# A Conformer block on one core: the first two query groups attend in two key halves, the front is ordered by its first chunk, two VectorE exponentials are in flight, and dummy matmuls stand in TensorE's waits

## The chip, the cores and the metric

The kernel runs on one core of a Trainium2 chip. The metric is the device time of one execution in microseconds (us). Before the change it was 1018.75, 1017.7 and 1015.3 us in three runs, a median of 1017.7 us. The profile is one further execution.

The core has five engines, each with its own in-order stream of instructions: TensorE (PE: matmuls into the accumulators in PSUM, with its weight loads shown apart as PEld), VectorE (DVE), ScalarE (ACT), GpSimd (POOL) and SyncE (SP, which only issues DMAs here). They wait for each other with semaphores.

## The reference, cut to what matters

B = 2 sequences of T = 4000 tokens with D = 144 features, H = 4 heads of 36, FF = 576, a depthwise convolution over 5 tokens; all in bfloat16.

```
h = layernorm(x);  x = x + 0.5 * (silu(h @ w_ff1a) @ w_ff1b)
h = layernorm(x);  q, k, v = heads(h @ w_qkv)
p = softmax(q @ k^T / 6);  x = x + (p @ v) @ w_o
h = layernorm(x) @ w_pw1;  h = h[:, :D] * sigmoid(h[:, D:])
c = depthwise_conv5(h);    x = x + silu(c) @ w_pw2
h = layernorm(x);  x = x + 0.5 * (silu(h @ w_ff2a) @ w_ff2b)
return layernorm(x)
```

Attention is the bulk: 2 x 4 x 4000 x 4000 scores, each of which needs an exponential.

## The kernel before

**Tiling.** The 8000 tokens are 16 chunks `c` of 500 (8 per sequence; CPB = 8), each chunk 4 blocks of 125 tokens. A chunk is also a query group. Keys come in 63 tiles of 64 (NT = 63), so attention is 16 x 63 = 1008 tiles, in the order of the list `its` (chunk, then key tile). One tile holds all four heads, in 128 partitions by 1000 columns:

- four score matmuls (`PS<-QT,KT`) fill two PSUM banks out of six (0 to 5) that all work shares;
- the exponential goes to one of the slots of the ring `PT` (NPT = 7). It is made by ScalarE in one instruction (`ACTIVATE PT<-PS 128x1000`), or by VectorE in eight (`dve_tile`, line 981, over the buffers `ZB` and `MB`): two that turn scores into a scaled integer (`ZB<-PS`), five that split it into exponent and mantissa and work out a polynomial, and a product that writes `PT`. At most one such VectorE tile is under way;
- four matmuls (`PS<-PT,VA`) add the tile's share of p @ v, with a column of ones that gives the softmax sum, into banks 6 and 7 (BX = 6), which no other work may use before the end.

After a chunk's last tile `epilogue` (line 927) copies banks 6 and 7 to `OTF` in one VectorE instruction, transposes it on TensorE (`PS<-IDF,OTF`), and normalises it to `AN`. Then `post1` does w_o, a layernorm and the gated product, and `post2` the convolution, w_pw2, the second feed-forward, the last layernorm and the store. A chunk's `pre` (line 755) is the first feed-forward (`ff1`: layernorm to `XN`, transposes by `IDENT` to `XT`, matmuls `PS<-XT,WA` and `PS<-XT,WE`, the silu to `HT`, matmuls `PS<-WB,HT`) and then `pre2` (line 730: layernorm, transposes to `XTQ`, projections to `KT`, `VA`, `QT`).

**Who sets the order.** The Python code does not write engine streams directly. Each piece of work is a generator (a thread) that asks for an engine, a bank or a slot (`need`), and `Rec.op` (line 67) records an instruction and estimates its end from a table of costs. `pick` (line 1071) chooses what is recorded next: scores "S", a ScalarE exponential "E", a p @ v "O", or a thread "T"; score matmuls are put off until `act_end() - 0.48`, the time at which ScalarE would run dry. `due` (line 1144) starts a VectorE tile. `replay` then writes the per-engine streams with semaphores, so that nearly all instructions of the profile carry one helper's line, L158; tiles are told apart by their names.

**Front and tail.** Until keys and values of all 8 chunks of the first sequence are made (`kv_done`), the mode is "front": a query group may only use the key tiles that are there, and no VectorE tile may start. The first group, chunk 0, needs all 63 key tiles, and with them the keys of chunks 1 to 7, before chunk 1 can begin (its sums would need banks 6 and 7). Chunks 0 and 1 use the silu of ScalarE's table (NSILU = 2), the later ones tanh, which shares a table with the exponential; changing tables is an `ACT_TABLE_LOAD`. In layernorms VectorE makes mean and variance (`ST`, `MV`), GpSimd adds epsilon and takes the power -0.5 (`RS`); `XN` is written by VectorE in front and tail, by GpSimd between. After the last exponential the mode is "tail": what is left is chunk 15's epilogue, `post1` and `post2`, beside the end of chunk 14's.

**Start.** The inputs' DMAs go out on SP (`X` of chunks 0 to 7, then other weights) and on ScalarE's queue (group w0: `WA`, `WE`, `WB`; group w1: `WQKV`). VectorE sets buffers to zero, then `setup_qk` (line 476) copies `WQKV` to the padded `WQ` and `WK`, and then the layernorm statistics begin. TensorE begins with 36 matmuls (NWARM) of a zeroed `PT` slot, whose results nobody uses.

Of the kernel before, what the change touches and what calls it, by code (L numbers as in the profile page):

```python
# [6 lines left out]
ALU = mybir.AluOpType  # L7
# [7 lines left out]
DH = 36  # L15
# [33 lines left out]
class Rec:  # L49
# [8 lines left out]
    def __init__(self, nc):  # L58
        self.nc = nc
        self.ops = []  # L60
        self.n = {}
        self.hist = {}
        self.free = {e: 1.0 for e in self.ENGS}
        self.kind = None
        self.last = 0.0

    def op(self, eng, name, *a, r=(), w=(), q=None, cost=0.1, kind=None, lat=None, **k):
# [4 lines left out]
        o.idx = self.n.get(lane, 0)  # L72
        self.n[lane] = o.idx + 1
# [11 lines left out]
        start = self.free[eng]  # L85
        for d, raw in o.deps:
            if d.eng != eng or d.q is not None or (raw and eng != "pe"):
                start = max(start, d.done + self.SEM[eng])
# [6 lines left out]
        o.done = start + cost + ((self.LAT[eng] if lat is None else lat) if q is None else 2.0)  # L95
# [213 lines left out]
def bass_standalone__conformer_family_zipformer__speech_kernel(  # L309
# [30 lines left out]
    NPT = 7  # L340
    NU = 5
    NAN = 5
    ND = 1
    NWARM = 36
    NSILU = 2
# [3 lines left out]
    ALONE = 2  # L349
    OFREE = 3  # L350
# [3 lines left out]
    LATE = 0.3  # L354
    DGAP = 4.0
# [8 lines left out]
    NHALF = sb("NHALF", [NB], F32)  # L364
    XT = sb("XT", [NXT, 2, CH])
# [8 lines left out]
    ZB = sb("ZB", [ND, 2, CH], U16)  # L374
    MB = sb("MB", [ND, 2, CH], U16)
# [32 lines left out]
    ZBF = ZB[:, :, :, :].rearrange("p a b n -> p (a b n)").bitcast(BF16).rearrange("p (a n) -> p a n", a=ND)  # L408
    MBH = MB[:, :, :, :].rearrange("p a b n -> p (a b n)").bitcast(F16).rearrange("p (a n) -> p a n", a=ND)

# [3 lines left out]
    def load(eng, q, dst, src, w):  # L414
        op(eng, "dma_start", dst, src, q=q, w=w, cost=0.7)
# [4 lines left out]
    def load_x(eng, c):  # L420
        load(eng, f"x{c}", X[0:TB, c * NB:(c + 1) * NB, :], x_tok[c], [("X", c, i) for i in range(NB)])

    def load_ff(eng, q, WA, WE, WB, wa, wb, nm):
        load(eng, q, WA[0:HD, :, :], kh(wa)[:, :, 0:512], [(nm, "a", 0)])
        load(eng, q, WE[0:HD, :, 64:128], kh(wa)[:, :, 512:FF], [(nm, "a", 1)])
        load(eng, q, WB[:, 0:4, :], wb[0:512, :].rearrange("(t p) d -> p t d", p=128), [(nm, "b", 0)])
        load(eng, q, WB[0:64, 4, :], wb[512:FF, :], [(nm, "b", 1)])
        load(eng, q, WB[64:128, 5, :], wb[512:FF, :], [(nm, "b", 2)])

    op("dve", "memset", WP2Z[:, :, :], 0.0, w=[("WP2Z", i) for i in range(NB)])  # L430
    load_x("sp", 0)
    load_ff("act", "w0", WA1, WE1, WB1, w_ff1a, w_ff1b, "W1")
    load("act", "w1", WQKV[0:HD, :, :], kh(w_qkv), ["WQKV"])
    for c in range(1, CPB):
        load_x("sp", c)
# [6 lines left out]
    load_ff("sp", "w2", WA2, WE2, WB2, w_ff2a, w_ff2b, "W2")  # L442
# [3 lines left out]
    op("dve", "memset", PT[:, 0, :, :], 0.0, w=[("PT", 0)])  # L446
# [3 lines left out]
    op("pool", "memset", NHALF[:, :], -0.5, w=["NHALF"])  # L450
    for WE, WB, nm in ((WE1, WB1, "W1"), (WE2, WB2, "W2")):
# [19 lines left out]

    for i in range(NWARM):
        op("pe", "matmul", PSV[:, i % 8, 0:CH], lhsT=PT[:, 0, 0, 0:128], rhs=PT[:, 0, 0, 0:CH], start=True, stop=True,
           r=[("PT", 0)], w=[("ps", i % 8)], cost=0.3)

    def setup_qk():
        for Wt, nm, o0 in ((WQ, "WQ", 0), (WK, "WK", D)):
            for k in range(2):
                op("dve", "tensor_copy", Wt[0:HD, k, :, 0:DH],
                   WQKV[0:HD, k, o0:o0 + D].rearrange("p (h d) -> p h d", h=H), r=["WQKV", nm + "0"], w=[nm],  # L480
                   cost=0.15)
# [4 lines left out]
    xnp, xtp, thp, htp, swp, anp, ptp, dzp = (  # L486
        Slots(R, range(n)) for n in (NXN, NXT, NTH, NHT, NSW, NAN, NPT, ND))
# [65 lines left out]
    def ln(c, bs):  # L553
# [8 lines left out]
        yield need("pool")  # L562
        op("pool", "tensor_scalar", RS[0:TB, u, 1, 0:n], MV[0:TB, u, 0:n, 1], LN_EPS, None, op0=ALU.add,
# [663 lines left out]
```

## Time and profile before

| what | value |
|---|---|
| median of three runs | 1017.7 us (1015.3 to 1018.75) |
| the profiled execution, its own time | 1012.16 us |
| its span in the trace | 1010.4 us (1.76 us lie around it) |
| mean granted TensorE clock | 0.976 |
| exponential tiles on ScalarE / VectorE | 906 / 102 |
| first exponential begins / last one ends | 39.32 / 964.65 us |

The page of the profile gives busy times by engine, the span in 40 slices, the chain of work that ended last, and the costliest groups of instructions. A group row reads: line, engine, operation, output tile<-input tiles, shapes, count | busy us, mean ns of one | idle time of the engine before them and what ended it. Since ScalarE's instructions overlap at their ends, the mean of one can be above busy time divided by count. A timeline row reads: start, duration, engine, line, operation, shapes, count, and in brackets the idle time before it with what ended it. A row of windows reads: the stretch, its length, busy time of PE, PEld, DVE, ACT and POOL with the number of instructions, the granted clock of TensorE, the DMA share and GB/s; where only PE was asked for, only its busy time stands there. The page's row PEclk is that clock in tenths for each slice, 9 being 90% or more.

### The profile page before, as it was taken

What the parts mean: (1) busy time and instruction counts of PE and PEld (TensorE: products, weight loads), DVE (VectorE), ACT (ScalarE), POOL (GpSimd) and SP (SyncE); (2) the same over time, 40 slices, a digit from 0 to 9 for tenths busy, and PEclk for the clock granted to TensorE, in tenths of its full rate; (3) what the DMA queues carried; (4) which work ended last, traced back from release to release, by engine and by line L of the source; (5) the groups of instructions that cost most, each with busy time, mean ns of one, the idle gap of its engine ahead of it and who ended that gap; (6) DMA issues with size and microseconds to landing.
All of it is one profiled execution on the core that took longest, in us unless ns stands there. A gap on an engine that the chain in (4) does not pass through costs nothing.

```text
span 1010.4 us, 26729 instructions
## 1 busy us (share of the span) xinstructions
PE 920.5 (91%) x11294; PEld 400.8 (40%) x11294; DVE 824.1 (82%) x2160; ACT 932.0 (92%) x1163; POOL 288.8 (29%) x563
## 2 busy tenths in 40 slices
PE   8999899999999999999999998799898998989865
PEld 4544244433444444434434343233333333334343
DVE  5976878997988888988879878888878887878745
ACT  3898889999999999999999999999999999999933
POOL 3321314324324325133523321111222231313213
PEclk8999989999999999999999999999999999999967
DMA  4000000000000000000000000000000000000000
GB/s 129 5 2 2 2 2 2 2 2 2 2 2 3 7 8 7 1 2 8 8 2 2 8 7 7 2 2 7 1 3 6 2 7 1 8 2 7 1 7 12
DMA packets 7290, 7.32 MB, mean 7 GB/s; under 512 B 2344, under 2 KB 7170, under 8 KB 7170
## 3 DMA queue, kind: packets, MB, share of 16 engines
q1 hardware_dynamic: 6014, 5.14, 1.7%
q8 instruction: 88, 1.44, 0.6%
q10 hardware_dynamic: 1156, 0.47, 0.2%
q14 instruction: 32, 0.26, 0.1%
HBM read 3.31 MB, written 2.30 MB: 6 GB/s over the span
## 4 chain that ended last, share of the span: by engine, by line
ACT 47%; PE 33%; DVE 12%; POOL 6%; issue 1%; DMA 1%; ACTq 0%; POOLq 0%; DVEq 0%
ACT PT L158 41%; PE PS L158 33%; ACT TH L158 6%; POOL XN L158 3%; POOL RS L158 3%; DVE MB L158 2%; DVE ZB L158 2%; DVE ST L158 2%; DVE X L158 1%; DVE HT L158 1%; DVE XT L158 1%; DMA WQKV<-in_w_qkv_dram 1%; DVE MV L158 1%; DVE PT L158 0%; DVE OTF L158 0%
## 5 line engine op out<-in xcount | busy, mean ns | idle before, releaser
L158 ACT ACTIVATE PT<-PS 128x1000 bf16<-128x1000 f32 x906 | 841.0, 1054 | 13.4 <-PE PS L158 12.0
L158 PE MATMUL PS<-QT,KT 64*64 64x500 bf16 x4032 | 419.9, 387 | 28.2 <-ACT PT L158 22.2
L158 PE MATMUL PS<-PT,VA 64*37 64x500 bf16 x4032 | 355.5, 376 | 16.5 <-ACT PT L158 13.3
L158 POOL TENSOR_SCALAR RS<-MV 125x4 f32<-125x4 f32 (+1 forms) x159 | 50.1, 315 | 643.1 <-DVE MV L158 637.8
L158 PEld LDWEIGHTS PS<-QT,KT 64*64 64x64 bf16 x4032 | 125.5, 104 | 225.8 <-ACT PT L158 146.6
L158 DVE TENSOR_SCALAR ZB<-PS 128x500 uint16<-128x500 f32 x204 | 137.7, 675 | 54.0 <-PE PS L158 50.1
L158 PEld LDWEIGHTS PS<-PT,VA 64*37 64x37 bf16 x4032 | 114.9, 95 | 132.1 <-ACT PT L158 49.1
L158 POOL TENSOR_SCALAR XN<-X,RS 125x144 bf16<-125x144 bf16 x232 | 124.6, 549 | 6.1
L158 ACT ACTIVATE TH<-PS 128x500 bf16<-128x500 f32 (+2 forms) x200 | 104.4, 549 | 10.0 <-PE PS L158 9.3
L158 POOL TENSOR_TENSOR RS<-RS,NHALF 125x4 f32<-125x4 f32 (+1 forms) x101 | 100.6, 996 | 8.4
L158 DVE SCALAR_TENSOR_TENSOR HT<-TH,PS 128x500 bf16<-128x500 bf16 (+1 forms) x140 | 83.4, 616 | 17.1 <-ACT TH L158 15.9
L158 DVE TENSOR_SCALAR MB<-MB 128x1000 f16<-128x1000 f16 x204 | 84.7, 415 | 1.7
L158 DVE SCALAR_TENSOR_TENSOR X<-PS,X 125x288 bf16<-125x288 f32 x128 | 57.2, 453 | 35.3 <-PE PS L158 34.3
L158 PE MATMUL PS<-XT,WA 72*128 72x500 bf16 x256 | 76.9, 396 | 4.7 <-DVE HT L158 3.1
L158 DVE BATCH_NORM_STATS2 ST<-X 125x6 f32<-125x144 bf16 x320 | 75.2, 293 | 0.2
L158 DVE TENSOR_TENSOR PT<-ZB,MB 128x1000 bf16<-128x1000 bf16 x102 | 70.6, 692 | 2.4
L158 DVE TENSOR_TENSOR MB<-MB 128x1000 f16<-128x1000 f16 x102 | 69.0, 676 | 2.1
L158 PE MATMUL PS<-WB,HT 128*125 128x144 bf16 x640 | 63.4, 239 | 1.1 <-ACT HT L158 0.7
L158 PEld LDWEIGHTS PS<-WB,HT 128*125 128x125 bf16 x640 | 49.3, 142 | 28.6 <-issue 18.6
L158 PE MATMUL PS<-IDENT,XN 125*72 125x125 bf16 x512 | 44.1, 227 | 17.8 <-DVE XN L158 9.0
L158 DVE COPY XT<-PS 72x1000 bf16<-72x1000 bf16 (+1 forms) x67 | 41.2, 616 | 17.7 <-PE PS L158 16.8
L158 PEld LDWEIGHTS PS<-IDENT,XN 125*72 125x72 bf16 x512 | 32.9, 116 | 39.8 <-POOL XN L158 14.4
(78 smaller groups left out, 687.0 us busy)
## 6 DMA issues: line engine op xcount, KB each, us to landing
X<-in_x_dram SPq DMA_DIRECT2D x16, 140.6 KB
out_dram<-XN SPq DMA_DIRECT2D x14, 140.6 KB
out_dram<-XN SPq DMA_DIRECT2D x4, 70.3 KB
WA<-in_w_ff1a_dram ACTq DMA_DIRECT2D x1, 144.0 KB
WB<-in_w_ff1b_dram ACTq DMA_DIRECT2D x1, 144.0 KB
WA<-in_w_ff2a_dram SPq DMA_DIRECT2D x1, 144.0 KB
WB<-in_w_ff2b_dram SPq DMA_DIRECT2D x1, 144.0 KB
WQKV<-in_w_qkv_dram ACTq DMA_DIRECT2D x1, 121.5 KB
```

The lines of the kernel that those rows point to most:

```text
L158: ins = getattr(eng, o.name)(*o.a, **o.k)
```

## The change

**Two key halves.** The list of tiles is built from `phases`: (chunk 0, key tiles 0 to 38), (chunk 1, 0 to 38), (chunk 0, 39 to 62), (chunk 1, 39 to 62), then chunks 2 to 15 whole (`NQ` = 2, `HALF` = 5 chunks of keys, 39 tiles). After a first half, `epilogue` copies banks 6 and 7 to `SAVE` (fp32, in space of `QT` that belongs to the second sequence) and ends; after the second half `OTF` is the sum of the banks and `SAVE`. Query projections that would overwrite `SAVE` wait until it has been read. Two chunks' queries, not one, are projected early.

**VectorE tiles.** `ZB` and `MB` go; a VectorE tile works in place in two slots of `PT`, of which there are now 9. Two tiles may be under way (`LIVE` = 2), the second from when the first has taken its scores (`early`); a tile near the end of its phase goes ahead of other threads (rank -1). They may begin in the front once 4 chunks of keys are made (`FDVE`). There are 899 exponentials on ScalarE and 109 on VectorE.

**Front.** Chunk 0's threads have rank -1 and go ahead of others that could begin up to `FIRST` = 0.3 earlier, until the first exponential. Only chunk 0 uses the silu table (`NSILU` = 1); tiny activations of `DUM` bring the silu table in at the start and the exponential's table after chunk 0's first feed-forward. `setup_qk` moves from VectorE to GpSimd and into `pre2` of chunk 0. The DMA of `X` for chunk 1, and with it all behind it on SP, waits for `WA` and `WE`; `WB` gets a queue of its own (w3). In front and tail, epsilon is added by VectorE, not GpSimd. On ScalarE, 146 `TH` (tanh) instructions of 500 columns stand where there were 142, 12 `HT` (silu) where there were 16; between the first and the last exponential it has 8 more `TH` of 500 columns, one more of 250, and on balance three more copies from PSUM.

**Dummy matmuls.** The 36 start matmuls become 50 of `IDENT` by `IDENT`, 128 columns. In `Rec.op`, `filler` puts more of them wherever TensorE is expected to wait over 0.12 us, until the first exponential (169 of them in all by then) and again in the tail (245). They write bank 7.

**Numbers of the planner.** The costs of DMAs, scores, p @ v, `XN_COST` and the power change, and scores are put off until `act_end() - AHEAD` with 0.64 in the place of 0.48.

The core of the diff:

```diff
@@ Rec.op
-        start = self.free[eng]
+        start = ready = self.free[eng]
...
+        if eng == "pe" and self.filler is not None and not self.filling:
+            self.filling = True
+            for _ in range(int((ready - start - 0.12) / 0.056)):
+                self.filler()
...
-    NPT = 7
+    NPT = 9
-    NWARM = 36
-    NSILU = 2
+    LIVE = 2
+    NWARM = 50
+    NSILU = 1
+    NQ = 2
+    FDVE = 4
+    SOON = 3
+    AHEAD = 0.64
+    HALF = 5
+    FIRST = 0.3
...
+    load_x("sp", 0)
+    load_ff("act", "w0", "w3", WA1, WE1, WB1, w_ff1a, w_ff1b, "W1", 3.5, 4.5)
+    load("act", "w1", WQKV[0:HD, :, :], kh(w_qkv), ["WQKV"], lat=5.0)
+    for c in range(1, CPB):
+        load_x("sp", c, [("W1", "a", 0), ("W1", "a", 1)] if c == 1 else ())
...
+    def warm(cost=0.056, bk=BX + 1, n0=0):
+        op("pe", "matmul", PSV[:, bk, n0:n0 + 128], lhsT=IDENT[:, :], rhs=IDENT[:, :], start=True, stop=True, r=["ID"],
+           w=[("ps", bk)], cost=cost, kind="f")
+
     for i in range(NWARM):
-        op("pe", "matmul", PSV[:, i % 8, 0:CH], lhsT=PT[:, 0, 0, 0:128], rhs=PT[:, 0, 0, 0:CH], start=True, stop=True,
+        warm(0.1, BX + i % 2, i // 2 % 4 * 128)
+    R.filler = warm
...
-                op("dve", "tensor_copy", Wt[0:HD, k, :, 0:DH],
+                op("pool", "tensor_copy", Wt[0:HD, k, :, 0:DH],
...
+        if silu and mode["front"] and c == NSILU - 1:
+            op("act", "activation", DUM[:, :], NHALF[:, 0:1], ACT.Exp, bias=0.0, scale=1.0, r=["NHALF"], w=["DUM"],
...
+    def epilogue(c, part):
+        if part:
+            op("dve", "tensor_copy", SAVE[:, c, :, :], ps, r=rk, w=[("SAVE", c), "OREL"], cost=c_dve(2 * CH))
...
+        if c < NQ:
+            op("dve", "tensor_tensor", OTF[:, :, :], ps, SAVE[:, c, :, :], op=ALU.add, r=rk + [("SAVE", c)],
...
+    phases = [(c, t0, t1) for t0, t1 in ((0, tiles_by(HALF - 1)), (tiles_by(HALF - 1), NT)) for c in range(NQ)]
+    phases += [(c, 0, NT) for c in range(NQ, NCH)]
...
-        deadline = act_end() - 0.48
+        deadline = act_end() - AHEAD
...
-        if n >= NIT or not DVE_EXP or len(kv_done) < CPB or live_dve[0] >= 1 or lag():
+        if n >= NIT or not DVE_EXP or live_dve[0] >= LIVE or early[0] or lag():
...
     mode["tail"] = True
-    for i in (BX, BX + 1):
-        banks.free[i] = R.last
+    banks.free[BX] = R.last
+    R.filler = warm
```

What this does to three places of the engine streams follows. A row is an instruction, or several alike in succession; "waits" names the semaphore that the first of them waits for.

**TensorE at the start.** Before, the start matmuls are followed by chunk 0's and chunk 1's transposes (`IDENT,XN`) and feed-forward:

```order
L158 MATMUL PS<-PT 128x500 x36
L158 MATMUL PS<-IDENT,XN 72x125 x12
L158 MATMUL PS<-XT,WA 128x500 x8
L158 MATMUL PS<-XT,WE 128x250 x4
L158 MATMUL PS<-IDENT,XN 72x125 x8
L158 MATMUL PS<-WB,HT 125x144 x20
```

Now:

```order
L167 MATMUL PS<-IDENT 128x128 x106
L167 MATMUL PS<-IDENT,XN 72x125 x4
L167 MATMUL PS<-IDENT 128x128 x2
L167 MATMUL PS<-IDENT,XN 72x125 x4
L167 MATMUL PS<-IDENT 128x128 x9
L167 MATMUL PS<-XT,WA 128x500 x8
L167 MATMUL PS<-XT,WE 128x250 x4
L167 MATMUL PS<-IDENT,XN 72x125 x4
L167 MATMUL PS<-IDENT 128x128 x8
L167 MATMUL PS<-WB,HT 125x144 x20
```

Chunk 1's transposes no longer stand ahead of chunk 0's first feed-forward matmul, and dummies fill the places between.

**VectorE at the start**, behind its memsets. Before, with s_q_w1, s_q_x0 to s_q_x2 the arrivals of `WQKV` and of `X` of chunks 0 to 2:

```order
L158 COPY WQ<-WQKV 72x4x36 [waits s_q_w1]
L158 COPY WQ<-WQKV 72x4x36
L158 COPY WK<-WQKV 72x4x36 x2
L158 BN_STATS ST<-X 125x6 [waits s_q_x0]
L158 BN_STATS ST<-X 125x6 x3
L158 BN_AGGR MV<-ST 125x2 [waits s_dve] x4
L158 BN_STATS ST<-X 125x6 [waits s_q_x1]
L158 BN_STATS ST<-X 125x6 x3
L158 BN_AGGR MV<-ST 125x2 [waits s_dve] x4
L158 BN_STATS ST<-X 125x6 [waits s_q_x2]
L158 BN_STATS ST<-X 125x6
L158 TENSOR_SCALAR XN<-X,MV,RS 125x144 [waits s_pool]
```

Now:

```order
L167 BN_STATS ST<-X 125x6 [waits s_q_x0]
L167 BN_STATS ST<-X 125x6 x3
L167 BN_AGGR MV<-ST 125x2 [waits s_dve] x2
L167 TENSOR_SCALAR RS<-MV 125x2 [waits s_dve]
L167 BN_AGGR MV<-ST 125x2 x2
L167 TENSOR_SCALAR RS<-MV 125x2 [waits s_dve]
L167 BN_STATS ST<-X 125x6 [waits s_q_x1]
L167 BN_STATS ST<-X 125x6
L167 TENSOR_SCALAR XN<-X,MV,RS 125x144 [waits s_pool]
```

The weight copies are gone from VectorE, so its first wait is for `X` of chunk 0; the first `XN` now stands behind the arrival of chunk 1's `X`, whose DMA on SP waits for `WA` and `WE`.

**TensorE at the last tiles.** Before, the last p @ v matmuls are followed by the epilogue's transposes:

```order
L158 MATMUL PS<-WB,HT 125x144 x5
L158 MATMUL PS<-PT,VA 37x500 x8
L158 MATMUL PS<-IDF,OTF 125x128 x8
L158 MATMUL PS<-IDENT,AN 72x125 x8
L158 MATMUL PS<-WO,XT 125x144 x8
L158 MATMUL PS<-IDENT,XN 72x125 x8
```

Now (`WB,HT` here is the end of chunk 14's second feed-forward):

```order
L167 MATMUL PS<-PT,VA 37x500 x8
L167 MATMUL PS<-IDENT 128x128 x26
L167 MATMUL PS<-IDF,OTF 125x128 x4
L167 MATMUL PS<-WB,HT 125x144 x15
L167 MATMUL PS<-IDF,OTF 125x128 x4
L167 MATMUL PS<-WB,HT 125x144 x5
L167 MATMUL PS<-IDENT 128x128 x9
L167 MATMUL PS<-IDENT,AN 72x125 x8
```

26 dummies now stand between the last p @ v and the transposes, and since they write bank 7, the first of them waits, like the transposes, for the VectorE copy to `OTF` that reads that bank. Chunk 14's matmuls stand between the two groups of transposes.

More of the change, by code (lines that the diff above doesn't have):

```diff
@@ L683, in proj @@
         cc = c % CPB
[L684 removed]
+        over = nm == "WQ" and p == 1 and c >= CPB
+        bk = yield need("pe", banks, dur=0.42, cond=(lambda: not saved) if over else None)
         for k in range(2):
@@ L689, in proj @@
         yield need("dve", hold=True)
-        copy(dst, PSV[:, bk, 0:CH], [("ps", bk)], [(nm + "T", c)], CH)
+        copy(dst, PSV[:, bk, 0:CH], [("ps", bk)], [(nm + "T", c)] + [("SAVE", i) for i in range(NQ) if over], CH)
         banks.give(bk)
@@ L1167, in bass_standalone__conformer_family_zipformer__speech_kernel @@
             live_dve[0] += 1
+            early[0] += 1
+            owed[0] += 2
             last_dve[0] = R.free["pe"]
-            S.add(dve_tile(n), R.free["pe"] - 0.3, first=True, rank=3)
+            th = S.add(dve_tile(n), R.free["pe"] - 0.3, first=True, rank=3)
+            tiles.append((th, n - its[n][2] + phases[its[n][0]][2]))
+        for th, end in tiles:
+            if n_s[0] >= end - SOON:
+                th.rank = -1
         banks.keep = KEEP
```

213 lines of the change are left out of this document (123 added, 90 removed).

## The prediction

> **What bounds the kernel now.** I read the page first, then windows by stage, then the groups, then the timeline of the first 40 us and of the end. From the page:
>
> ```profile
> span 1010.4 us, 26729 instructions
> PE 920.5 (91%) x11294; PEld 400.8 (40%) x11294; DVE 824.1 (82%) x2160; ACT 932.0 (92%) x1163; POOL 288.8 (29%) x563
> PEclk8999989999999999999999999999999999999967
> ACT 47%; PE 33%; DVE 12%; POOL 6%; issue 1%; DMA 1%; ACTq 0%; POOLq 0%; DVEq 0%
> ```
>
> Two engines are over 90% busy, and the chain of waits goes 47% over ScalarE and 33% over TensorE. The mean hides three stages; the windows cut at the first and the last exponential (39.3 and 964.65), with two pieces of the middle:
>
> ```profile
> 0.00:39.30 39.30, 33.09 (x246) 19.31 (x246) 28.04 (x131) 18.45 (x33) 13.59 (x35) 0.91 0.29 85
> 39.30:112.50 73.20, 70.32 (x916) 32.00 (x916) 56.50 (x184) 64.98 (x89) 17.18 (x37) 1.00 0.01 2
> 112.50:150.00 37.50, 32.70 (x350) 13.32 (x342) 29.96 (x89) 31.40 (x37) 8.59 (x15) 0.86 0.00 1
> 39.30:964.65 925.35, 860.11 (x10869) 362.94 (x10868) 773.16 (x1937) 901.86 (x1109) 263.62 (x501) 0.99 0.01 4
> 964.65:1010.40 45.75, 27.35 (x184) 18.50 (x182) 22.89 (x93) 11.69 (x23) 11.54 (x28) 0.66 0.04 10
> ```
>
> In the middle ScalarE is busy 901.86 of 925.35 us (97%), so that stage is ScalarE's work plus 23.5 us of idle time: 8.2 up to 112.5, 6.1 up to 150, 9.2 in all the rest. The front (39.3) and the tail (45.75) are chains of dependent steps in which no engine is full. So 85 us lie outside the bound engine's work, plus 23.5 of idle, and the change goes after these; it takes little work off ScalarE.
>
> **The change part by part. (1) The front.** The timeline of the start:
>
> ```profile
> 1.74 9.96 PE L158 MATMUL PS<-PT 128*128 128x500 bf16 x36 [1.74 <-DVE PT L158]
> 3.75 0.56 ACTq L158 DMA_DIRECT2D WQKV<-in_w_qkv_dram  x1
> 10.44 0.30 DVE L158 COPY WQ<-WQKV 72x144 bf16<-72x144 bf16 x2 [5.29 <-DMA WQKV<-in_w_qkv_dram]
> 10.87 0.93 DVE L158 BATCH_NORM_STATS2 ST<-X 125x6 f32<-125x144 bf16 x4
> 14.08 0.41 PE L158 MATMUL PS<-IDENT,XN 125*72 125x125 bf16 x4 [2.38 <-DVE XN L158]
> 16.05 3.13 PE L158 MATMUL PS<-XT,WA 72*128 72x500 bf16 x8
> 16.72 1.28 ACT L158 ACT_TABLE_LOAD   x1
> 18.01 2.42 ACT L158 ACTIVATE HT<-PS 128x500 bf16<-128x500 f32 x5
> 22.70 1.06 DVE L158 SCALAR_TENSOR_TENSOR X<-PS,X 125x288 bf16<-125x288 f32 x2 [0.34 <-PE PS L158]
> 23.05 1.98 PE L158 MATMUL PS<-XT,WA 72*128 72x500 bf16 x8
> 27.37 0.81 DVE L158 SCALAR_TENSOR_TENSOR X<-PS,X 125x288 bf16<-125x288 f32 x2
> 31.75 1.41 PE L158 MATMUL PS<-WB,HT 128*125 128x144 bf16 x20
> 33.45 0.58 ACT L158 ACTIVATE XTQ<-PS 72x500 bf16<-72x500 bf16 x1 [0.91 <-PE PS L158]
> 37.15 0.59 ACT L158 ACTIVATE QT<-PS 128x500 bf16<-128x500 f32 x1 [0.64 <-DVE QT L158]
> 38.02 1.28 ACT L158 ACT_TABLE_LOAD   x1
> 39.32 6.38 ACT L158 ACTIVATE PT<-PS 128x1000 bf16<-128x1000 f32 x7
> ```
>
> VectorE waits 5.29 us for `WQKV` before any statistics. With the weight copies on GpSimd, statistics can start from about 5 (the trace doesn't show when chunk 0's `X` lands; the upper bound is 10.87). Two things keep this from being all gain. The first `XN` stands behind chunk 1's `X`, whose DMA now goes out only when `WA` and `WE` have landed; nothing shows these times, so they are bounded by no wait at all and by twice the at most 6.1 us of `WQKV` (from 4.31 to 10.44), counted from `WE`'s issue, which precedes it by some 2.6: 13.9. And 106 dummies precede the first transposes: 36 of 500 columns took 9.96, or 0.071 us per 128 columns, so 106 take at least 7.5, and end at 9 to 10.3 when they start near 1.5. Between the two I take the dummies' time, put the first transposes at 9.5 to 10 and the first `WA` matmul at 11.4 (10.5 to 12.5), for 14.08 to 16.05 took 2.0 with chunk 1's share in between. That is 4.6 us before the 16.05 of now. Then `WA` to the residual `X` took 7.7 us for chunk 0 (16.05 to 23.76), with half clock and a table load, and 5.1 for chunk 1 (23.05 to 28.18). By the second, chunk 0's `X` is ready at 16.5. From there to the first exponential is 15.6 us now (23.76 to 39.32), with chunks 1 and 2 going ahead and a table load at the end. Alone, two layernorm halves, transposes and `XTQ` take some 4.5 us (the first layernorm's 3.2 from 10.87 to 14.08, plus transposes and copy), and from `XTQ` to the exponential's scores 33.45 to 38.02 is 4.6. That makes 25.6, and 25.8 with the statistics of chunks 1 to 3 that VectorE has between. **Term: -13.5** (ends -9, with the late `X`, and -16). The moved copies cost GpSimd nothing that waits: it is busy 13.59 of 39.30. SP's wait holds back chunks 2 to 7 and other weights; they are needed later than chunk 1 and cost nothing.
>
> [...]
>
> **(2) The middle.** ScalarE's work by group:
>
> ```profile
> L158 ACT ACTIVATE PT<-PS 128x1000 bf16<-128x1000 f32 x906 | 841.0, 1054 | 13.4 <-PE PS L158 12.0
> L158 ACT ACTIVATE TH<-PS 128x500 bf16<-128x500 f32 x142 | 85.4, 625 | 8.6 <-PE PS L158 8.2
> ```
>
> An exponential costs 841.0 / 906 = 0.93, a `TH` 85.4 / 142 = 0.60. Seven exponentials leave (-6.5), but an earlier first exponential means that front work now lies after it: 8 `TH` of 500 columns (+4.8), one of 250 and three copies (about +1.9). The sum is 0: 902 us. What can shrink is idle time. The stretch from 112.5 to 150 shows one dip; windows of TensorE alone, and GpSimd's row there:
>
> ```profile
> 122.00:124.00 2.00, 0.11 (x4) 1.00 0.00 0
> 126.00:130.00 4.00, 3.31 (x21) 0.50 0.00 0
> 130.00:136.00 6.00, 6.00 (x47) 0.51 0.00 0
> 121.42 2.54 POOL L158 TENSOR_SCALAR XN<-X,RS 125x144 bf16<-125x144 bf16 x4
> ```
>
> When the front ends, TensorE waits for the first GpSimd layernorms of the second sequence, stands nearly still for 2 us, and then runs at half clock for 10, being full from 130 to 136. With a VectorE tile allowed in the front and the keys complete at tile 78 in place of 54, that moment has more tiles in hand; I take half of the dip away (3). The 8.2 of the front part shrinks by 2.5 or not at all: its work gets denser. Until 112.5 TensorE does 33.09 - 9.96 + 70.32 = 93.5 us of work; 24 more tiles at some 0.8 us each make 112, which from 11.4 is over at 123 if it never waits; ScalarE would have some 93 of 97 us there. **Term: -5.5** (ends +6 and -16: no dip goes and the dense part loses 6 more, or the late idle time of 9.2 halves too). VectorE's cover gets thinner:
>
> ```profile
> L158 DVE TENSOR_SCALAR ZB<-PS 128x500 uint16<-128x500 f32 x204 | 137.7, 675 | 54.0 <-PE PS L158 50.1
> L158 DVE TENSOR_SCALAR MB<-MB 128x1000 f16<-128x1000 f16 x204 | 84.7, 415 | 1.7
> L158 DVE COPY OTF<-PS 128x1000 f32<-128x1000 f32 x16 | 19.2, 1198 | 5.2 <-PE PS L158 4.8
> ```
>
> Eight instructions of 0.42 to 0.68 make a tile of about 4.4, so 7 tiles add 31, and two partial copies 2.4: VectorE goes from 773 to some 810 of 920 us (88%). It holds p @ v back for 1.2 us at each of two more phase ends; with two exponentials' worth of `PT` slots more, ScalarE goes on meanwhile: nothing, or 2.4 if the ring is full.
>
> **(3) The tail.** Three windows of it, and the epilogue's start in the timeline:
>
> ```profile
> 968.80:974.60 5.80, 2.27 (x16) 1.83 (x16) 4.30 (x22) 0.58 (x1) 3.39 (x7) 0.50 0.00 0
> 981.20:986.40 5.20, 5.20 (x32) 3.65 (x32) 0.02 (x1) 1.14 (x3) 0.01 (x1) 0.55 0.02 5
> 992.10:1000.10 8.00, 7.98 (x43) 5.36 (x44) 1.88 (x7) 3.31 (x6) 0.76 (x2) 0.54 0.00 0
> 965.47 1.20 DVE L158 COPY OTF<-PS 128x1000 f32<-128x1000 f32 x1
> 966.72 1.14 PE L158 MATMUL PS<-IDF,OTF 128*125 128x128 f32 x8 [1.31 <-DVE OTF L158]
> ```
>
> Convolution and last feed-forward run on a full TensorE at half clock. At full clock the 5.2 become about 2.9 and the 8.0 about 4.7 (there ScalarE and VectorE take over the pace, with 3.3 and 1.9 us of work); half of the 2.27 in the first window is 1.1 more. That is 6.7. Given back: the 26 dummies ahead of the transposes, released by the same copy: at full clock 8 matmuls of 500 columns took 1.98 (23.05), so 128 columns take 0.063 and 26 of them 1.6. Chunk 14's 15 `WB` matmuls between the two groups of transposes take 1.1 (20 took 1.41), of which VectorE's work on the first group hides some: 0.6. **Term: -4.5** (ends -1 and -7). If the dummies don't keep the clock, the term is +2.
>
> **Sum:** -13.5 - 5.5 - 4.5 = -23.5. Against the profiled execution: 1012.16 - 23.5 = 988.7, a span of 987. That execution lies 5.5 below the median; against the median of 1017.7 it is **994**.
>
> **The rivals.** *More idle time goes (981).* The later deadline for scores (0.64 for 0.48) and two VectorE tiles in flight take most of the late 9.2 and all of the dip: the middle gives some -16, the rest as above. For it speaks that 12.0 of the 13.4 us of idle time before exponentials end with a score matmul; against it that TensorE is 93% busy in the middle. *The dense part gives it back (1006).* After 25.8 TensorE, VectorE and ScalarE are all nearly full until the keys are complete; TensorE was at 96% from 39.3 to 112.5, and at 96% the 112 us take 117. Then idle time rises by 6 where I let it fall by 5.5. *It does not do what it says (1018).* Chunk 1's late `X` and the dummies hold the front near 32, the keys come as late as ScalarE can use them, and the tail's dummies cost what the clock brings: within 0.3%, about 3 us, which is what a measurement of this kernel can tell from no change. *Slower (1030).* VectorE is in order; with two tiles in flight up to eight tile instructions, 4.4 us, can stand ahead of a copy (`XT`, `HT`, `KT`) for which TensorE waits, as it did near 122. A pause like that cost 6.1 us of ScalarE's time with the half clock behind it. Fewer than four more such pauses leave a gain; from five on the change is slower, and six make 1030. For it speaks VectorE at 88%; against it that VectorE waits 54 us for scores now, so its tiles seldom press. [...]
>
> **How the numbers follow.** My forecast 0.54, own range 983 to 1003 (the terms' ends, partly cancelling); more idle time gone 0.16 (977 to 985); given back 0.12 (1003 to 1013); no change 0.07; slower 0.11. Faster by over 0.3% is the first three, 0.82. From 978 to 1013 all but no change, slower and a sliver is held.
>
> **What would show it.** Right: the first exponential near 25.8, `WA` near 11.4 in full clock; 900 to 904 us of ScalarE's work in the middle with 16 to 20 idle; no 2 us pause of TensorE where the keys are complete; a tail of 40 to 43 with the clock at 1.00 and a stretch of 1.6 of dummies between `OTF` and the transposes. Wrong: a first exponential after 29, idle time over 25 in the middle, or half clock in the tail in spite of the dummies.

## The result and the profile after

The changed kernel takes 990.71 us (990.47 to 990.94, four runs) where the kernel before takes 1016.5 (1015.13 to 1018.75): a ratio of 0.9744, with a 95% interval of 0.9723 to 0.9765. The profiled executions differ by less, since that of before was among its faster ones: 1010.4 to 988.6 of span, 21.8 us. The page of the changed kernel, with the rows that answer to those of before:

```profile
span 988.6 us, 27456 instructions
PE 923.5 (93%) x11672; PEld 418.0 (42%) x11672; DVE 836.8 (85%) x2260; ACT 924.2 (93%) x1159; POOL 298.5 (30%) x525
PEclk9999999999999999999999999999999999999999
ACT 56%; PE 29%; DVE 11%; POOL 3%; issue 1%; POOLq 0%; DVEq 0%
```

ScalarE's part of the chain of waits has grown from 47% to 56%, and the two slow slices at the end of the PEclk row are gone. The same windows as before, cut at the first and the last exponential of this kernel:

```profile
0.00:25.24 25.24, 23.52 (x300) 19.35 (x300) 19.72 (x98) 11.94 (x23) 7.99 (x20) 1.00 0.45 123
25.24:112.50 87.26, 81.58 (x1003) 37.34 (x1001) 73.72 (x256) 79.08 (x111) 16.07 (x23) 1.00 0.02 5
112.50:150.00 37.50, 32.83 (x430) 11.58 (x428) 26.77 (x71) 34.60 (x41) 9.63 (x14) 0.95 0.01 2
25.24:945.92 920.68, 865.75 (x10935) 369.31 (x10933) 792.07 (x2058) 900.18 (x1114) 281.42 (x487) 1.00 0.01 4
945.92:988.60 42.68, 34.23 (x441) 29.38 (x441) 25.00 (x106) 12.08 (x25) 9.12 (x18) 0.93 0.04 11
```

| stage | before | after | difference | predicted |
|---|---|---|---|---|
| up to the first exponential | 39.32 | 25.24 | -14.1 | -13.5 |
| first to last exponential | 925.33 | 920.68 | -4.7 | -5.5 |
| after it | 45.75 | 42.68 | -3.1 | -4.5 |

A second way to cut the span serves the experiments better: ScalarE's busy time over the whole span, and its idle time by stage (the length of a window less ScalarE's busy time in it). The five numbers of a row add up to its span, within rounding. The changed kernel stands there twice: its second profile is that of *after_again* below, the slowest of four further runs.

| kernel | ScalarE's work | idle to first exp. | idle to 150 | idle to last exp. | idle in the tail | span |
|---|---|---|---|---|---|---|
| before | 932.0 | 20.9 | 14.3 | 9.2 | 34.1 | 1010.4 |
| after | 924.2 | 13.3 | 11.1 | 9.4 | 30.6 | 988.6 |
| after, second profile | 925.0 | 13.9 | 12.7 | 12.5 | 29.0 | 993.0 |
| no tail dummies | 924.2 | 13.0 | 11.4 | 9.4 | 35.3 | 993.3 |
| tail dummies in a free bank | 924.1 | 13.1 | 11.3 | 9.3 | 27.6 | 985.3 |
| no dummies in front waits | 924.9 | 18.9 | 10.7 | 10.1 | 30.6 | 995.2 |
| one VectorE tile | 940.3 | 13.8 | 8.4 | 11.4 | 28.7 | 1002.6 |
| scores at 0.48 | 922.6 | 13.0 | 9.0 | 24.0 | 28.5 | 997.1 |
| whole groups | 917.2 | 13.3 | 13.7 | 13.3 | 28.5 | 986.0 |
| no precedence | 921.0 | 14.4 | 4.1 | 10.8 | 28.9 | 979.2 |
| two chunks ahead | 918.4 | 16.2 | 9.4 | 16.1 | 29.4 | 989.5 |
| free bank, early X | 925.8 | 11.3 | 9.0 | 18.8 | 27.4 | 992.3 |

The two profiles of the changed kernel run the same instructions and differ by up to 3.1 us of idle time in a stage, so a smaller difference between two rows shows nothing by itself. Between the first two rows the change saves 7.8 of work (7 exponentials at 0.93 and a table load of 1.28, of which there are 3 where there were 4, come to that), 7.6 of idle time in the front, 3.2 up to 150 and 3.5 in the tail. The front's -14.1 is thus half a saving; the other half is work that moved behind the first exponential.

### The profile page after: what moved, and what is told of

Its sections match the earlier page's. It is cut to its first block, busy times and chain, and to the rows that moved or that the text cites. A ratio compares the mean times of both kernels' runs of the same rounds, so it can differ in the third digit from the quotient of the medians.

```text
span 988.6 us, 27456 instructions
## 1 busy us (share of the span) xinstructions
PE 923.5 (93%) x11672; PEld 418.0 (42%) x11672; DVE 836.8 (85%) x2260; ACT 924.2 (93%) x1159; POOL 298.5 (30%) x525
## 4 chain that ended last, share of the span: by engine, by line
ACT 56%; PE 29%; DVE 11%; POOL 3%; issue 1%; POOLq 0%; DVEq 0%
ACT PT L167 50%; PE PS L167 29%; ACT TH L167 6%; DVE PT L167 5%; POOL XN L167 2%; POOL RS L167 1%; DVE ST L167 1%; DVE HT L167 1%; DVE XT L167 1%; DVE X L167 1%; DVE OTF L167 0%; DVE AN L167 0%; DVE MV L167 0%; DVE QT L167 0%; ACT HT L167 0%
## 5 line engine op out<-in xcount | busy, mean ns | idle before, releaser
L167 ACT ACTIVATE PT<-PS 128x1000 bf16<-128x1000 f32 x899 | 839.0, 1063 | 15.7 <-PE PS L167 13.8
L167 PE MATMUL PS<-PT,VA 64*37 64x500 bf16 x4032 | 364.0, 377 | 6.4 <-ACT PT L167 2.9
L167 POOL TENSOR_SCALAR RS<-MV 125x4 f32<-125x4 f32 x116 | 39.0, 336 | 472.6 <-DVE MV L167 467.8
L167 DVE TENSOR_SCALAR PT<-PT 128x1000 uint16<-128x1000 uint16 (+1 forms) x436 | 177.1, 419 | 5.0
L167 DVE TENSOR_SCALAR PT<-PS 128x500 uint16<-128x500 f32 x218 | 145.9, 670 | 16.4 <-PE PS L167 15.3
L167 POOL TENSOR_SCALAR XN<-X,RS 125x144 bf16<-125x144 bf16 x232 | 146.2, 642 | 6.0
L167 DVE TENSOR_TENSOR PT<-PT 128x1000 f16<-128x1000 f16 (+1 forms) x218 | 145.6, 681 | 1.8
L167 ACT ACTIVATE TH<-PS 128x500 bf16<-128x500 f32 (+2 forms) x205 | 111.8, 570 | 3.2 <-PE PS L167 2.9
L167 DVE SCALAR_TENSOR_TENSOR HT<-TH,PS 128x500 bf16<-128x500 bf16 (+1 forms) x145 | 87.0, 616 | 27.2 <-ACT TH L167 26.3
L167 PE MATMUL PS<-XT,WA 72*128 72x500 bf16 x256 | 72.6, 379 | 3.0 <-DVE HT L167 2.6
L167 PEld LDWEIGHTS PS<-IDENT,XN 125*72 125x72 bf16 x512 | 31.4, 112 | 26.7 <-issue 11.4
L167 POOL COPY U<-U 128x2 bf16<-128x2 bf16 (+1 forms) x56 | 12.6, 256 | 79.2 <-DVE U L167 79.2
```

Source lines behind the costliest of these rows:

```text
L167: ins = getattr(eng, o.name)(*o.a, **o.k)
```

## The experiments

**The tail's dummies.** In the timeline and the TensorE windows of the changed kernel (first profile; *half clock* is a granted clock of 0.50):

```profile
946.42 1.20 DVE L167 COPY OTF<-PS 128x1000 f32<-128x1000 f32 x1 [0.69 <-PE PS L167]
947.68 2.43 PE L167 MATMUL PS<-IDENT 128*128 128x128 bf16 x26 [1.31 <-DVE OTF L167]
949.91 1.16 PE L167 MATMUL PS<-IDF,OTF 128*125 128x128 f32 x4
948.00:949.00 1.00, 1.00 (x16) 0.65 0.00 0
949.00:950.00 1.00, 1.00 (x12) 0.50 0.00 0
951.00:952.00 1.00, 1.00 (x13) 0.65 0.00 0
```

The 26 dummies wait for the copy. They begin at 947.68, the clock falls to half at about 948.3 (0.65 is the mean of that window), and they take 2.43 us. Four runs bear on it.

*tail_none*: `R.filler = warm` behind the last exponential is left out.

```diff
     banks.free[BX] = R.last
-    R.filler = warm
```

> The changed kernel without its dummy matmuls after the last exponential; every other instruction is as in the changed kernel (990.7 us, tail 42.7 us from the last exponential to the end). Theory: the dummies hold the clock, which is worth 6.7 us, and the 26 ahead of the transposes cost 2.4. Without them the tail shows a clock near 0.6 again and lasts 47 us, so 995. Rival: the tail got shorter by its order and by epsilon on VectorE, and the dummies only cost: tail 40 to 41, time 988 to 989.

996.06 us (995.09 to 997.54; ratio to before 0.9843, 0.9814 to 0.9873). Its tail:

```profile
945.51:993.30 47.79, 28.77 (x196) 20.00 (x196) 24.99 (x106) 12.54 (x25) 9.10 (x18) 0.66 0.03 10
```

A tail of 47.8 at a clock of 0.66, as the theory had it: the dummies are worth 5.1 us net. Without them the tail is longer than the 45.75 before the change, so the rival, that order and epsilon shortened it, falls.

*tail_late*: no dummies until the last normalisation.

```diff
-    R.filler = warm
+    R.filler = lambda: warm() if o_done[0] else None
```

> The changed kernel without the 26 dummies ahead of the last transposes; the later dummies stay. Theory: these 26 (2.43 us at half clock) stand on the path behind the copy of the sums, and what follows them runs at half clock either way: 2.2 us less, tail 40.5, time 988.5. Rival: they bring the clock up for the matmuls behind them, so that without them the half clock lasts as much longer: tail 42.5 to 43.5, time 990.5 to 991.5.

990.17 us (986.17 to 991.05; 0.9773, 0.9742 to 0.9803). The four runs fall into two sorts: one of 986.17 with a mean clock of 0.996, which is the profiled one, and three of 990.13 to 991.05 with 0.991 to 0.992. In the profile the clock of the tail is 1.00 in every window from 944.71 to 960, and the mean of 0.94 in the last row comes from what follows. In the changed kernel's first profile it is 1.00 from 952 to 984, with the last matmul ending at 981.65, and 0.50 from 986 to the end. Of *tail_late*:

```profile
944.71:947.00 2.29, 0.93 (x8) 0.64 (x9) 1.52 (x2) 0.27 (x2) 0.00 (x0) 1.00 0.00 0
947.00:949.00 2.00, 2.00 (x31) 2.00 (x30) 1.46 (x5) 0.00 (x0) 0.00 (x0) 1.00 0.00 0
944.71:984.40 39.69, 31.18 (x415) 26.33 (x415) 25.00 (x106) 12.08 (x25) 9.10 (x18) 0.94 0.04 12
```

In that execution the tail is 3.0 us shorter than in the changed kernel's first profile; the median gains nothing that can be told. The three slower runs were not profiled, so where they lost their clock is not shown. Neither side is borne out as stated; the next run takes the pause away.

*tail_free*: the same dummies at the same places, but in a bank that is free, so that they run during the copy.

```diff
-    R.filler = warm
+    def warm_free():
+        ok = [i for i in banks.free if i < BX and banks.free[i] <= R.free["pe"]]
+        if ok:
+            warm(bk=min(ok, key=lambda i: (banks.free[i], i)))
+    R.filler = warm_free
```

> The changed kernel with the dummies of the tail written to a bank among 0 to 5 that is free, not to bank 7, in the same order and number. So the 26 ahead of the transposes no longer wait for the copy of the sums and run beside it. Theory: the pause of 1.3 us before them is what lets the clock fall, and their wait is what puts them on the path. Both go: clock 1.00 through the tail, tail 39.5 to 40, time 987.5 to 988. Rival: the clock falls in spite of it, because what went before (945 to 947) was sparse: tail 41 to 42, time 989 to 990.

987.33 us (987.07 to 987.7; 0.9731, 0.9704 to 0.9757), beside *after_again*, the changed kernel in the same group:

> The changed kernel itself once more, beside the others of this group on the same chip. Every theory: 988 to 991 us, the clock near 0.993, the tail 42 to 43 us with the half clock from about 948 to 951 as before, or, where the clock happens not to fall there, 39 to 40 and 987.

That took 991.17 us (990.21 to 994.78; 0.9765, 0.9733 to 0.9797): the range of its four runs is wider than was expected of them. Its slowest run, 994.78, has the lowest mean clock, 0.988, and is the profiled one. There the half clock lies elsewhere: from 55.2 to 62.1 and, by the PEclk row of its page, in the slice from 893.7 to 918.5 (mean below 0.90), but not on the dummies of the tail, although they come behind the same pause:

```profile
953.68 1.62 PE L167 MATMUL PS<-IDENT 128*128 128x128 bf16 x26 [1.31 <-DVE OTF L167]
951.92:993.00 41.08, 32.59 (x441) 27.74 (x441) 24.99 (x106) 12.08 (x24) 9.10 (x18) 0.97 0.04 12
```

Of tail_free:

```profile
946.03 1.62 PE L167 MATMUL PS<-IDENT 128*128 128x128 bf16 x26
946.15 1.20 DVE L167 COPY OTF<-PS 128x1000 f32<-128x1000 f32 x1 [0.69 <-PE PS L167]
947.49 0.65 PE L167 MATMUL PS<-IDF,OTF 128*125 128x128 f32 x4
945.65:985.30 39.65, 32.53 (x441) 27.74 (x441) 24.99 (x106) 12.08 (x25) 9.10 (x18) 0.96 0.04 12
```

The dummies take 1.62 beside the copy, the transposes follow 0.14 after it ends, and the tail is 39.65. The theory held for the time and for the clock: dummies and transposes run at the full clock (1.62 for 2.43, 0.65 for 1.16), and its mean over the tail is 0.96 for 0.93. But of the 3.0 us against the first profile only 1.4 (41.08 to 39.65) are the wait; the other 1.6 are the half clock, which does not come in every execution.

**The dummies of the front.** *front_nofill* keeps the 50 at the start and leaves out those in the waits.

```diff
     for i in range(NWARM):
         warm(0.1, BX + i % 2, i // 2 % 4 * 128)
-    R.filler = warm
```

> The changed kernel with the 50 start dummies but without the 119 put into waits before the first exponential; the order of all else is as in the changed kernel (first exponential at 25.2 us). Theory: the clock falls to half before chunk 0's first feed-forward, which then takes what it took before the change (3.1 and 1.0 us for 1.9 and 0.6), and the projections too: first exponential 2.5 to 3 later, time 993.5. Rival: the clock is full anyway once real work starts, and the 106 dummies up to 9.8 us only hold the transposes up: first exponential 0.4 earlier or equal, time 990 to 990.7.

996.6 us (995.08 to 998.79; 0.9845, 0.9818 to 0.9873).

```profile
10.72 3.49 PE L167 MATMUL PS<-XT,WA 72*128 72x500 bf16 x8 [0.60 <-DVE XT L167]
31.59 1.90 ACT L167 ACTIVATE PT<-PS 128x1000 bf16<-128x1000 f32 x2 [2.62 <-PE PS L167]
0.00:31.59 31.59, 25.00 (x181) 16.89 (x181) 20.50 (x101) 12.68 (x22) 7.97 (x20) 0.71 0.37 106
```

The first feed-forward matmul starts as early (10.72), but at half clock, and the clock is 0.71 over the whole stage. The first exponential comes 6.35 us later, double what the theory gave. I had counted only what the feed-forward and part of the projections lose; by windows of 2 us the clock is half from 9.6 to 19.8 and again from 23.2 to 33.4, over all of the projections and the first scores.

**VectorE tiles in flight.** *live1*:

```diff
-    LIVE = 2
+    LIVE = 1
```

> The changed kernel with one VectorE exponential tile in flight in the place of two. The planner then gives VectorE 93 tiles and ScalarE 915 (109 and 899 with two). Theory: ScalarE's work sets the time between the first and the last exponential, and idle time stays near 20 us, so 16 more exponentials of 0.93 us cost 15: time 1005. Rival 1: a second tile in flight takes about as much back by queueing on VectorE as it adds, so idle time falls by 8 or more with one: time under 998. Rival 2: idle time grows as well: over 1009.

1003.63 us (1003.37 to 1004.45; 0.9915, 0.989 to 0.9939).

```profile
25.71:962.12 936.41, 870.49 (x10951) 372.67 (x10949) 755.74 (x1932) 916.56 (x1130) 271.05 (x487) 1.00 0.01 4
```

ScalarE's work rises by 16.4 us and its idle time stays (19.9 for 20.5): the middle follows the number of exponentials on ScalarE, as the theory had it (1005). This is the largest effect of a single edit here, 12.5 us against the 991.17; with one tile VectorE gets 93, fewer than the 102 of before.

**When scores are due.** *ahead48*:

```diff
-    AHEAD = 0.64
+    AHEAD = 0.48
```

> The changed kernel with scores put off until 0.48 before ScalarE runs dry, as before the change, in the place of 0.64. The planner then gives ScalarE 889 exponentials (899) and VectorE 119. Theory: with the later scores ScalarE waits for TensorE more often: its work falls by 9.3 us, its idle time between the first and last exponential rises from 20.5 to about 28, time 989. Rival 1: idle time stays at 20.5, time 981.5: the 0.64 was a loss. Rival 2: idle time rises by more than 12, time over 993: the 0.64 is one of the change's gains.

997.97 us (996.69 to 999.22; 0.9835, 0.9806 to 0.9864): the second rival. Ten exponentials fewer on ScalarE, and idle time from 150 on of 24.0 for 9.4. The list of TensorE's waits, with total us, number and longest, first of this kernel:

```profile
PE PS L167 <- POOL XN L167: 11.9, 13, 2.6
PE PS L167 <- POOL U L167: 4.7, 5, 2.7
```

and of the changed kernel:

```profile
PE PS L167 <- POOL XN L167: 5.0, 5, 2.0
```

In this list, with scores put off longer, TensorE more often reaches work that GpSimd has not released; that this is all of the difference is not shown.

**The key halves.** *nohalf*, and *tf_nohalf* with the tail's dummies in a free bank besides:

```diff
-    phases = [(c, t0, t1) for t0, t1 in ((0, tiles_by(HALF - 1)), (tiles_by(HALF - 1), NT)) for c in range(NQ)]
-    phases += [(c, 0, NT) for c in range(NQ, NCH)]
+    phases = [(c, 0, NT) for c in range(NCH)]
```

> The changed kernel with whole query groups, as before the change; all else of it stays. The planner then gives ScalarE 889 exponentials and VectorE 119. Theory: without the halves there are too few tiles in hand while the keys are made; ScalarE's idle time from the first exponential to 150 rises from 11.1 us to 22 or more, which the 9.3 us of work less does not make up: 992 to 997. Rival: the reordered front alone keeps ScalarE fed; idle time there stays near 11, time 981 to 984, and the halves gave nothing.

> The changed kernel with the tail's dummies in a free bank (987.3 us) and with whole query groups, as before the change. Theory: the halves gain nothing in the middle (ScalarE 7 us less work, idle time 7 more), and the dip of the clock near 130 goes with them: time 985 to 987, tail 39.6. Rival 1: the two add up in full, 984 or less. Rival 2: the 988 us without halves came from a tail whose clock happened to hold, so nothing is left: 988 or more.

987.93 us (986.11 to 988.1; 0.9732, 0.9704 to 0.976) beside the 991.17 of the changed kernel, and 986.4 (984.85 to 988.22; 0.9726, 0.9699 to 0.9754) against 987.33 for the free bank alone. Of nohalf:

```profile
25.26:150.00 124.74, 115.41 (x1427) 52.58 (x1425) 107.06 (x357) 111.06 (x152) 28.58 (x44) 1.00 0.01 3
150.00:944.95 794.95, 750.58 (x9508) 318.99 (x9508) 716.93 (x1773) 781.61 (x958) 254.08 (x444) 1.00 0.01 4
```

Idle time up to 150 is 13.7, not 22: my theory of the first of them fell, and its rival's time (981 to 984) was not reached either. The one of the second held for the time, and against the first profile for its parts: 7 us less work and 6.5 more idle time up to the last exponential (1.3 more against the second). Without the halves the kernel is 3.2 us faster beside the 991.17, and with the free bank 0.9, inside the ranges. The halves, the first part of the change, give nothing that these runs can tell.

**Precedence of chunk 0.** *front_order*:

```diff
-    FIRST = 0.3
+    FIRST = 0.0
-        if mode["front"] and not stats["exp"] and not (got[1] == "T" and got[2].rank < 0):
+        if FIRST and mode["front"] and not stats["exp"] and not (got[1] == "T" and got[2].rank < 0):
-        S.add(pre(c, c < NSILU), rank=-1 if c == 0 else 1)
+        S.add(pre(c, c < NSILU))
```

> The changed kernel (990.7 us, first exponential at 25.2) without chunk 0's precedence in the front; dummies, tables, halves and all else stay. The planner then sets the feed-forwards of chunks 1 and 2 ahead of chunk 0's keys, and gives ScalarE 895 exponentials (899). Theory: the first exponential comes some 6 us later, at 31, but the work ahead of it need not be done later, and of the 6 us only 1 to 3 are left at the end: 991 to 994. Rival 1: all 6 come through, 996 to 997. Rival 2: it makes no difference where the work is done, 988 to 991.

981.01 us (980.77 to 981.26; 0.9673, 0.9643 to 0.9702): faster than all that was expected, and 1.0% faster than the changed kernel.

```profile
0.00:31.54 31.54, 29.91 (x380) 24.33 (x380) 26.74 (x132) 17.19 (x34) 10.84 (x24) 1.00 0.38 107
31.54:150.00 118.46, 113.36 (x1454) 48.37 (x1450) 104.46 (x318) 114.40 (x145) 20.95 (x33) 1.00 0.01 2
150.00:938.48 788.48, 745.14 (x9452) 319.14 (x9452) 697.55 (x1743) 777.66 (x955) 251.52 (x450) 1.00 0.02 4
```

The first exponential comes at 31.54, 6.3 later, and costs almost nothing: ScalarE does 5.25 us more work before it, so its idle time there grows by 1.1. From there to 150 idle time is 4.1 where the changed kernel has 11.1 (12.7 in its second profile), four exponentials move to VectorE (-3.2 of work in all), idle time after 150 is 1.4 more, and the tail has 1.7 less: there the clock did not fall, as it did not in the second profile of the changed kernel (28.9 and 29.0).

*front_two* asks whether that is a rule: precedence for two chunks.

```diff
-        S.add(pre(c, c < NSILU), rank=-1 if c == 0 else 1)
+        S.add(pre(c, c < NSILU), rank=-1 if c < 2 else 1)
```

> The changed kernel (990.7 us) with precedence in the front for chunks 0 and 1, not for chunk 0 alone: half way to the run without precedence, which took 981.0. The planner gives ScalarE 893 exponentials (899 in the changed kernel, 895 without precedence). Theory: ScalarE's time is its work plus its idle time, and a feed-forward done ahead of the first exponential is not done after it, where TensorE and VectorE are full; so the first exponential at 27 to 29 us costs nothing by itself, idle time before it stays at 13 to 14.5 us, idle time from there to 150 lies between the 11.1 of the changed kernel and the 4.1 without precedence, and with 5.6 us less work the time is 981 to 985. Rival 1: the run without precedence was fast because its list happens to have no pause of TensorE with half clock behind it later on; then this one keeps its 9 to 11 us of idle time up to 150, and any pauses after it, and takes 986 to 992. Rival 2: a later first exponential costs what it is late, and something else made up for it there: over 992.

991.37 us (991.3 to 995.27; 0.9797, 0.9773 to 0.9821). Its idle time is 16.2, 9.4 and 16.1 in the three stages up to the last exponential: the first rival. Fewer exponentials on ScalarE (893) are paid for by idle time all along. So the gain without precedence doesn't come in steps with the number of chunks let ahead.

**Chunk 1's X.** *tf_x1*, on top of the free bank:

```diff
-        load_x("sp", c, [("W1", "a", 0), ("W1", "a", 1)] if c == 1 else ())
+        load_x("sp", c, ())
```

> The changed kernel with the tail's dummies in a free bank (987.3 us) and, besides, with the DMA of chunk 1's X and those behind it sent at the start, not after WA and WE have landed. The planner then puts 57 dummies, not 106, ahead of the first transposes. Theory: the wait for chunk 1's X (1.9 us on VectorE) holds back the first XN, and goes: first feed-forward matmul at 9.3 in the place of 11.0, first exponential 1.5 to 2 us earlier, time 985 to 986. Rival: the X transfers share the way with WA and WE, which land later by as much, so that the first feed-forward matmul stays near 11 or comes later: 987 or more.

994.13 us (991.41 to 995.74; 0.9799, 0.977 to 0.9829).

```profile
9.52 1.87 PE L167 MATMUL PS<-XT,WA 72*128 72x500 bf16 x8
23.83 1.00 ACT L167 ACTIVATE PT<-PS 128x1000 bf16<-128x1000 f32 x1 [1.29 <-PE PS L167]
```

In the front the theory was near: 9.52 and 23.83, 1.2 us before the 24.99 of the free bank alone. The time is the rival's (987 or more), but not for its reason, since the first feed-forward matmul came early. The planner's list is another one from there on, and in it idle time from 150 on is 18.8. Three of its pauses (1.26, 2.04 and 2.05 us) end with the same copy; the last of them:

```profile
870.33 1.84 POOL L167 TENSOR_TENSOR RS<-RS,NHALF 125x4 f32<-125x4 f32 x1
874.58 1.41 POOL L167 COPY U<-U 128x2 bf16<-128x2 bf16 x4
876.05 0.39 PE L167 MATMUL PS<-U,DG 128*128 128x500 bf16 x1 [2.05 <-POOL U L167]
```

TensorE waits 2.05 us for a GpSimd copy behind a chain of GpSimd instructions that run beside those of VectorE tiles. Half clock and 1.7 us of idle ScalarE follow.

Not run one by one were the nine slots, the tables, the moved weight copies and the planner's costs.

## Why the prediction was right, point by point

The forecast was 994 for the median, 988.7 for a run as fast as the one profiled before; the changed kernel took 990.71, and 990.47 where it was profiled. Against either measure the gain lies some 2 us from the 23.5 of the sum (25.8 between the medians, 21.7 between the profiled runs).

**The front.** -14.1 for -13.5. The steps: first `WA` matmul at 10.99 (11.4 said), chunk 0's `X` ready at 15.97 (16.5), first exponential at 25.24 (25.8).

```profile
1.53 8.31 PE L167 MATMUL PS<-IDENT 128*128 128x128 bf16 x106 [1.53 <-POOL NHALF L167]
8.39 0.52 DVE L167 BATCH_NORM_STATS2 ST<-X 125x6 f32<-125x144 bf16 x2 [1.91 <-DMA X<-in_x_dram]
10.99 1.86 PE L167 MATMUL PS<-XT,WA 72*128 72x500 bf16 x8
25.24 2.79 ACT L167 ACTIVATE PT<-PS 128x1000 bf16<-128x1000 f32 x3 [1.29 <-PE PS L167]
```

Both delays named there are seen: VectorE waits 1.91 us for chunk 1's `X`, and the dummies end at 9.84. The division of the term was not right: of it I gave 2.6 us to the clock and a table load of chunk 0's feed-forward; the dummies in the waits alone are worth 6.35. Without them the new order brings the first exponential only to 31.59, at a clock of 0.71 where the kernel before had 0.91. I had not counted that this order, left alone, would lose clock; that the total came out so near is in part luck.

**The middle.** -4.7 for -5.5. ScalarE's work was put at 902 and is 900.2; idle time at 18 and is 20.5 (25.1 in the second profile, just over the 25 that I had named as a sign of being wrong). Half of the dip was to go, and it lost 2.9 us where it had lost 6.1; the 2.5 expected of the stretch up to 112.5 did not come (8.2 before and after), and 1.7 less work made up for most of that. One of the two reasons that I gave for the smaller dip, the keys complete at a later tile, is not borne out: without the halves the stretch from 112.5 to 150 has only 0.9 us of idle time, and the one before it 12.8 for 8.2. And the pause itself, which I said would not show, is still there, later:

```profile
138.00 3.99 POOL L167 TENSOR_SCALAR XN<-X,RS 125x144 bf16<-125x144 bf16 x4
142.05 0.63 PE L167 MATMUL PS<-IDENT,XN 125*72 125x125 bf16 x8 [1.98 <-POOL XN L167]
143.00:144.00 1.00, 1.00 (x16) 0.50 0.00 0
```

What the forecast left to a rival, without a price of its own, was the deadline for scores (it calls 0.64 the later one; with 0.64 scores come earlier). In the list that the planner writes with 0.48 the kernel takes 6.8 us more (997.97 against 991.17). As far as that is the deadline's own worth, the rest of the middle got worse by about as much, and the size of the term is luck. With 0.48 the time would have stayed in the range, 4.0 above the forecast, where it is now 3.3 below. Which part of the change needs the 0.64 was not run.

**The tail.** -3.1 for -4.5. In the first profile the 26 dummies take 2.43 us at half clock, not 1.6 at full, and the transposes behind them run at half clock too: the half clock in spite of the dummies that I had named as a sign of being wrong. In the second profile it does not come, the dummies take 1.62, and the tail is 41.08: -4.7. So the sum of this term was right for a full clock. What it left out is that the pause of 1.31 us ahead of the dummies can cost the clock, as it did in the first profile.

**The rivals.** More idle time gone: no, the late idle time stayed (9.2 before, 9.4 and 12.5 after), and the price given for this rival does not follow from its parts, -13.5 - 16 - 4.5 from 1017.7 being 984, not 981. The dense part giving it back: no, idle time up to 150 did not rise (14.3 to 11.1 and 12.7). Not doing what it says: no, the first exponential came at 25.24, not near 32, and the tail's dummies bring 5.1 net. Slower: the copies on VectorE that it named hold TensorE up for 0.6 us at most (0.8 before). What lies nearer to it is that `XN` instructions on GpSimd take longer,

```profile
L167 POOL TENSOR_SCALAR XN<-X,RS 125x144 bf16<-125x144 bf16 x232 | 146.2, 642 | 6.0
```

642 ns each for 549, and four of them took 3.99 beside a VectorE tile in the row at 138.00 where 1.79 was seen before. That VectorE tiles are what makes them longer is not shown: the mean does not follow the number of tiles, being 549 ns with the 102 of before, 616 with the 93 of *live1* and 642 with the 109 here. In the changed kernel two pauses of TensorE with half clock behind them, of 1.98 us at 142 and 1.22 at 694, end with such an `XN`.

**What the sum did not see.** The forecast did charge the work that moves behind the first exponential, some 6.7 us, to ScalarE in the middle. What the same move does to TensorE and VectorE there it left to the rival of the dense part. The run without precedence shows that it counts: with the feed-forwards of chunks 1 and 2 set ahead, the first exponential comes 6.3 us later and idle time up to 150 is 4.1 for 11.1. So the front's -13.5 was not a gain of that size; without the precedence that brings 6.3 of it, the kernel is faster. What stays open is how much of the 9.7 us without precedence is a rule and how much the particular list: it has idle time of 4.1 up to 150 with no half clock (1.00 in its windows there), and letting two chunks ahead gave none of it.

## What to carry to other kernels

Count the bound engine's idle time by stage over the whole span, not the moment at which it starts its main work: starting 6.3 us later with more done was 1% faster here. Dummy matmuls that keep the clock belong into a bank that nobody is reading, so that they fill the wait and are not released by it: here the tail was 39.65 us with them in a free bank, 41.08 and 42.68 with them in bank 7. Profile the same kernel twice before reading a few us of one stage: here the same instructions differed by 3.1. Where a planner writes the whole order, a small edit changes all of it; only edits whose order stays the same (the dummies here) measure their own worth.

## What the runs showed of the hardware

In these runs half clock followed pauses of TensorE of 1.2 to 2.1 us amid sparse matmuls: 1.98 ahead of 142.05, 1.22 ahead of 694.65 and 1.31 ahead of 947.68 in the first profile, 1.90 ahead of 124.01 before the change, 2.05 ahead of 876.05 in *tf_x1*. The stretches behind them lasted about 3.41 us or a whole number of times that: 3.4 in the tail above (948.30 to 951.71), 10.2 before the change (125.68 to 135.92); that of the second profile, 6.8 (55.24 to 62.08). Within each of two executions, measured over the whole span, the stretches begin on one grid: in the first profile at 142.76, 695.70 and 948.30, which lie 162 and 74 times 3.413 us apart, before the change at 125.68 and 968.77, 247 times. The second profile's 55.24 lies off the grid of the first, 25.6 times 3.413 us before its 142.76, and what a pause costs differs with it. The pause of 1.31 us in the tail, cut on the grid, first in the first profile, then in the second:

```profile
944.89:948.30 3.41, 1.68 (x23) 1.00 0.00 0
948.30:951.71 3.41, 3.41 (x31) 0.50 0.00 0
949.53:952.94 3.41, 2.42 (x26) 1.00 0.00 0
952.94:956.36 3.42, 2.68 (x42) 1.00 0.00 0
```

The first falls into one cell, which is left with 1.68 us of work, and the next cell is at half clock; the second is split between two cells, and the clock stays. Of the eight profiles here with these 26 dummies in bank 7, each behind a pause of 1.3 to 1.5 us, two show the half clock there. Busy time of a cell alone does not tell the two apart: in the first profile the clock stays behind a cell with 2.10 us of work (880.02 to 883.43), in the second the cell ahead of the half clock at 55.24 has at least 2.28 (of the 8 us from 48 to 56 TensorE is idle for 1.13). What sets the clock is not shown beyond this.
